# Routing attention and an MLP mixer on one core: cluster marks turned by a transposing DMA, the range check in three steps, a pair's x turned in one place

## The chip, the cores and the metric

The kernel runs on one core of a Trainium2 chip. The metric is the device time in microseconds (us), from the first instruction to the last; lower is better. Three runs of the kernel before gave 903.83, 905.47 and 905.58 us; their median, 905.47 us, is the time before.

## What is computed

Two blocks follow each other. The first is attention in which a query sees only the keys of its own cluster; the second mixes tokens and then channels. Cut to what matters:

```python
# q, k, v: (4, 8, 768, 64), 16 centroids for each head
q_assign = argmax(q_n . c_n)            # nearest of 16 centroids, k likewise
mask = q_assign[:, :, :, None] == k_assign[:, :, None, :]
scores = where(mask, (q @ k.T) / 8, -1e9)
attn = softmax(scores)
x = attn @ v                            # bridged to (4, 768, 512)
h = relu(x.T @ w_tok1) @ w_tok2         # tokens, 768 -> 256 -> 768
u = x + h.T
out = u + relu(u @ w_ch1) @ w_ch2       # channels, 512 -> 1536 -> 512
```

## The kernel before

The attention works on 16 pairs of heads (`NPAIR`), each in four steps (`GROUPS`): a step is one half of the queries (384 of 768) against three blocks of 128 keys. `m` counts the 64 steps, `g` is the pair and `s` the step in it. While pair `g` is in its scores, pair `g+1` is routed, which means that the nearest centroid of each of its queries and keys is found, and pair `g-1` is finished. Instructions run on each engine in the order in which the code gives them.

Routing compares each row's 16 similarities with their maximum. The result `oh` has rows as partitions; the scores need it turned, clusters as partitions (`ohT`). The turned marks enter the score as one more product in the same PSUM sum: a key's marks are 0 for its own cluster and -2^33 for the others, so a query of another cluster gets a score that the exponential takes to 0.

```python
    def route(g, a0=0, a1=2):

        st = state[g]
        NR = (a1 - a0) * NJ * 2
        sc = rsmall.tile([P, NR, C], F32, name="sim")
        nc.vector.transpose(
            out=sc.rearrange("p n c -> p (n c)"), in_=st.pop("pr")
        )
        mx = rsmall.tile([P, NR], F32, name="mx")
        nc.vector.reduce_max(out=mx, in_=sc, axis=AX.X)
        oh = ohs[g % 2][:, a0:a1].rearrange("p a j (h x) -> p (a j) h x", h=2)[:, :, :, 0:C]
        nc.vector.tensor_tensor(
            out=oh, in0=sc.rearrange("p (n h) c -> p n h c", h=2),
            in1=mx.rearrange("p (n h) -> p n h", h=2).unsqueeze(3).to_broadcast([P, NR // 2, 2, C]),
            op=ALU.is_ge,
        )

    def route_turn(g, a, po=None):

        st, oh = state[g], ohs[g % 2]
        if a == 1:
            st["ohT"] = qktp.tile([P, 2, NJ, P], BF16, name="ohT")
        if po is None:
            po = ps_sc.tile([P, NJ, P], BF16, tag="sc", name="po")
        for j in range(NJ):
            nc.tensor.transpose(out=po[:, j], in_=oh[:, a, j], identity=identb)
        st["po", a] = po

    def route_copy(g, a):
        st = state[g]
        po = st.pop(("po", a))
        if a == 0:
            nc.vector.tensor_copy(out=st["ohT"][:, 0], in_=po)
        else:
            nc.scalar.activation(
                out=st["ohT"][:, 1], in_=po, func=ACT.Copy, scale=BIG, bias=-BIG,
                accum_out=cells[:, g : g + 1],
            )
```

The scores of one step take three tiles of the PSUM pool `ps_sc`, which has `NG` = 3 buffers in all. The tile that is used last waits longest for its buffer, so its products come last:

```python
    def scores(m):
        g, qh, j0 = split(m)
        st = state[g]
        js = slice(HJ * qh, HJ * qh + HJ)
        scs = [ps_sc.tile([P, 2, 512], F32, tag="sc", name="sc") for _ in range(NG)]

        for chunks in (range(NG - 1), (NG - 1,)):
            for src, start in ((st["ohT"], True), (st["T"], False)):
                for i in chunks:
                    for h in range(2):
                        rows = slice(h * D, (h + 1) * D)
                        nc.tensor.matmul(
                            scs[i][:, h, 0:HS], lhsT=src[rows, 1, j0 + i], rhs=src[rows, 0, js],
                            start=start, stop=not start,
                        )
        for i in range(NG):
            ex = work.tile([P, 2, HS], F32, name="ex")
            nc.scalar.activation(out=ex, in_=scs[i][:, :, 0:HS], func=ACT.Exp, scale=SM_SCALE)
            st["ex", qh, j0 + i] = ex
```

A finished pair is turned back (`half_turn`, six transposes on PE in two halves) and divided by its sums into `x` (`half_out`, on DVE):

```python
    def half_turn(g, qh, px):
        for i in range(HJ):
            nc.tensor.transpose(
                out=px[:, i * P : i * P + P], in_=state[g]["avT"][:, HJ * qh + i], identity=ident
            )
        state[g]["px", qh] = px

    def half_out(g, qh):

        b, f = divmod(g, NF)
        nc.vector.tensor_tensor(
            out=xs[b][:, HJ * qh : HJ * qh + HJ, f * P : (f + 1) * P].rearrange(
                "p j (h d) -> p j h d", h=2
            ),
            in0=state[g].pop(("px", qh)).rearrange("p (j h d) -> p j h d", h=2, j=HJ),
            in1=rcps[:, g, qh].rearrange("p h j -> p j h").unsqueeze(3).to_broadcast([P, HJ, 2, D]),
            op=ALU.mult,
        )
# ... (half_out goes on:)
            in0=state[g].pop(("px", qh)).rearrange("p (j h d) -> p j h d", h=2, j=HJ),
            in1=rcps[:, g, qh].rearrange("p h j -> p j h").unsqueeze(3).to_broadcast([P, HJ, 2, D]),
            op=ALU.mult,
        )
```

The order of a pair's four steps (`add_up` sums the exponentials on DVE, `values` multiplies them with v on PE, `weights` holds the pieces in which the weights of the second block are prepared, on DVE, ACT and GpSimd):

```python
    for m in range(last + 3):
        g, s = divmod(m, GROUPS)
        more = g < NPAIR - 1
        old = g - 1 if m < last else -1
        if s == 2:
            if old >= 0:
                pair_denominators(old)
            if more:
                route(g + 1)
            if old >= 0:
                pair_reciprocals(old)
        if s == 3 and old >= 0:
            half_out(old, 0)
        if s == 0 and old >= 1:
            half_out(old - 1, 1)
        if more and s == 0:
            turn(g + 1)
        if 1 <= m <= last:
            add_up(m - 1)
        if m < last:
            scores(m)
        if 1 <= m <= last:
            values(m - 1)
        if m < last and s == 1:
            two = ps_sc.tile([P, 2, 512], F32, tag="sc", name="small")
            if old >= 0:
                pair_sums(old, two[:, 0, 0:HS])
            if more:
                route_products(g + 1, pr=two[:, 1, 0:HS])
        if m < last and s == 2:
            if more:
                two = ps_sc.tile([P, 2, 1024], BF16, tag="sc", name="po")
                for a in (1, 0):
                    po = two[:, a, 0 : NJ * P].rearrange("p (j t) -> p j t", j=NJ)
                    route_turn(g + 1, a, po)
                for a in (1, 0):
                    route_copy(g + 1, a)
            if old >= 0:
                half_turn(old, 0, ps_w.tile([P, HS], F32, tag="w", name="px"))
        if m < last and s == 3 and old >= 0:
            half_turn(old, 1, ps_w.tile([P, HS], F32, tag="w", name="px"))
        # ... (the end of the last pair)
        if s == 1 and g + 2 < NPAIR:
            load(g + 2)
        # ...
        if m < last - GROUPS:
            n = m % WEVERY == 0 or m == 1        # WEVERY = 3
        else:
            n = m % 2 if m < last else 2
        for _ in range(min(n, len(weights))):
            weights.pop(0)()
        # ...
```

The fast path holds for inputs in a certain range. `fits` finds out whether they were in it: 1/sum within limits, and one cluster only for each key. It counts over the partitions with a product on PE and loads the three counts into a register of every engine; if they fall short, a general version is run after the fast one.

```python

    def fits():

        inside = const.tile([P, 3, 2 * NPAIR * 2 * HJ], F32, name="inside")
        good = const.tile([P, 3], F32, name="good")
        flat = rcps.rearrange("p n i h j -> p (n i h j)")
        for i, (limit, op) in enumerate(((LIMIT, ALU.is_le), (1.0 / LIMIT, ALU.is_ge))):
            nc.vector.tensor_scalar(
                out=inside[:, i], in0=flat, scalar1=limit, scalar2=None, op0=op
            )
            nc.vector.tensor_reduce(out=good[:, i : i + 1], in_=inside[:, i], axis=AX.X, op=ALU.min)

        nc.vector.tensor_scalar(
            out=inside[:, 2, 0:NPAIR], in0=cells, scalar1=1.0 / BIG, scalar2=float(S),
            op0=ALU.mult, op1=ALU.add,
        )
        nc.vector.reduce_sum(out=good[:, 2:3], in_=inside[:, 2, 0:NPAIR], axis=AX.X)
        pn = ps_w.tile([1, 3], F32, tag="w", name="pn")
        nc.tensor.matmul(pn, lhsT=ones[:, 0:1], rhs=good, start=True, stop=True)
        count = const.tile([1, 3], I32, name="count")
        nc.vector.tensor_copy(out=count[:, 0:2], in_=pn[:, 0:2])
        nc.vector.tensor_scalar(
            out=count[:, 2:3], in0=pn[:, 2:3], scalar1=float(B * H * S), scalar2=float(P),
            op0=ALU.is_equal, op1=ALU.mult,
        )
        loaded = [
            nc.values_load(count[0:1, i : i + 1], min_val=0, max_val=P) for i in range(3)
        ]
# ... and in the second block:
            for i in range(3):
                ch2_chunk(b, part, i)
                # ...
            if b == 0 and part == 0:
                both = fits()
    late.pop()()          # the last product of the last chunk
    # ...
    with tc.If(both < 3 * P):
        general()
```

Of the kernel before, what the change touches and what calls it, by code (L numbers as in the profile page):

```python
# [8 lines left out]
F32 = mybir.dt.float32  # L9
BF16 = mybir.dt.bfloat16  # L10
U32 = mybir.dt.uint32
I32 = mybir.dt.int32
ALU = mybir.AluOpType
ACT = mybir.ActivationFunctionType
AX = mybir.AxisListType

B, H, S, D = 4, 8, 768, 64
C = 16
P = 128
# [28 lines left out]
def kernel(  # L48
# [257 lines left out]
    def route(g, a0=0, a1=2):  # L306

        st = state[g]  # L310
        NR = (a1 - a0) * NJ * 2
        sc = rsmall.tile([P, NR, C], F32, name="sim")
        nc.vector.transpose(
            out=sc.rearrange("p n c -> p (n c)"), in_=st.pop("pr")
        )
        mx = rsmall.tile([P, NR], F32, name="mx")
        nc.vector.reduce_max(out=mx, in_=sc, axis=AX.X)
        oh = ohs[g % 2][:, a0:a1].rearrange("p a j (h x) -> p (a j) h x", h=2)[:, :, :, 0:C]
        nc.vector.tensor_tensor(
            out=oh, in0=sc.rearrange("p (n h) c -> p n h c", h=2),  # L320
            in1=mx.rearrange("p (n h) -> p n h", h=2).unsqueeze(3).to_broadcast([P, NR // 2, 2, C]),
            op=ALU.is_ge,
        )

    def route_turn(g, a, po=None):

        st, oh = state[g], ohs[g % 2]
        if a == 1:
            st["ohT"] = qktp.tile([P, 2, NJ, P], BF16, name="ohT")
        if po is None:
            po = ps_sc.tile([P, NJ, P], BF16, tag="sc", name="po")
        for j in range(NJ):
            nc.tensor.transpose(out=po[:, j], in_=oh[:, a, j], identity=identb)  # L338
        st["po", a] = po

    def route_copy(g, a):
        st = state[g]
        po = st.pop(("po", a))
        if a == 0:
            nc.vector.tensor_copy(out=st["ohT"][:, 0], in_=po)  # L345
        else:
            nc.scalar.activation(
                out=st["ohT"][:, 1], in_=po, func=ACT.Copy, scale=BIG, bias=-BIG,
                accum_out=cells[:, g : g + 1],
            )  # L350


    def split(m):
# [284 lines left out]
    def ch2_chunk(b, part, i):  # L638
# [29 lines left out]

        chunk(DM // 2, product, done)

    def fits():

        inside = const.tile([P, 3, 2 * NPAIR * 2 * HJ], F32, name="inside")
        good = const.tile([P, 3], F32, name="good")
        flat = rcps.rearrange("p n i h j -> p (n i h j)")
        for i, (limit, op) in enumerate(((LIMIT, ALU.is_le), (1.0 / LIMIT, ALU.is_ge))):
            nc.vector.tensor_scalar(
                out=inside[:, i], in0=flat, scalar1=limit, scalar2=None, op0=op
            )
            nc.vector.tensor_reduce(out=good[:, i : i + 1], in_=inside[:, i], axis=AX.X, op=ALU.min)  # L680

        nc.vector.tensor_scalar(
            out=inside[:, 2, 0:NPAIR], in0=cells, scalar1=1.0 / BIG, scalar2=float(S),
            op0=ALU.mult, op1=ALU.add,
        )
        nc.vector.reduce_sum(out=good[:, 2:3], in_=inside[:, 2, 0:NPAIR], axis=AX.X)
        pn = ps_w.tile([1, 3], F32, tag="w", name="pn")
        nc.tensor.matmul(pn, lhsT=ones[:, 0:1], rhs=good, start=True, stop=True)
        count = const.tile([1, 3], I32, name="count")
        nc.vector.tensor_copy(out=count[:, 0:2], in_=pn[:, 0:2])  # L690
        nc.vector.tensor_scalar(
            out=count[:, 2:3], in0=pn[:, 2:3], scalar1=float(B * H * S), scalar2=float(P),
            op0=ALU.is_equal, op1=ALU.mult,
        )
        loaded = [
            nc.values_load(count[0:1, i : i + 1], min_val=0, max_val=P) for i in range(3)
        ]
        return loaded[0] + loaded[1] + loaded[2]


    def begin():
        cen = rsmall.tile([P, D], F32, name="cen")
        nc.sync.dma_start(cen, centroids.rearrange("h c d -> (h c) d"))
        load(0, (nc.scalar, nc.sync))

        nc.vector.memset(ones, 1.0)
        warm = rsmall.tile([P, WMAX], BF16, name="warm")
        nc.vector.memset(warm, 0.0)
        nc.scalar.activation(out=rsmall.tile([P, QP], F32, name="expd"), in_=ones, func=ACT.Exp)
        make_identity(nc, ident)  # L710
        nc.gpsimd.tensor_copy(out=identb, in_=ident)
        for oh in ohs:
            nc.gpsimd.memset(oh, 0.0)
        load(1)
        pw = ps_av.tile([P, HS], F32, name="av")

        def keep_warm(n):
            for _ in range(n):
                nc.tensor.matmul(pw, lhsT=warm[:, 0:P], rhs=warm[:, P : P + HS], start=True, stop=True)

        keep_warm(12)
        centroids_norm(cen)
        keep_warm(7)
        turn(0, (1,))
        route_products(0, 1, 2)
        turn(0, (0,))
        route(0, 1, 2)
        keep_warm(1)
        route_products(0, 0, 1)
        keep_warm(2)  # L730
        route_turn(0, 1)
        route_copy(0, 1)
        route(0, 0, 1)
        keep_warm(1)
        route_turn(0, 0)
        route_copy(0, 0)

    begin()
    weights = list(weight_steps(stage, W, ("tok1", "tok2", "ch1")))
# [7 lines left out]
# [9 lines that stand above are left out]
            if old >= 0:  # L756
                pair_reciprocals(old)
        if s == 3 and old >= 0:
            half_out(old, 0)
        if s == 0 and old >= 1:  # L760
            half_out(old - 1, 1)
        if more and s == 0:
            turn(g + 1)
        if 1 <= m <= last:
# [8 lines that stand above are left out]
                pair_sums(old, two[:, 0, 0:HS])  # L773
            if more:
                route_products(g + 1, pr=two[:, 1, 0:HS])
        if m < last and s == 2:
            if more:
                two = ps_sc.tile([P, 2, 1024], BF16, tag="sc", name="po")
                for a in (1, 0):
                    po = two[:, a, 0 : NJ * P].rearrange("p (j t) -> p j t", j=NJ)  # L780
                    route_turn(g + 1, a, po)
                for a in (1, 0):
                    route_copy(g + 1, a)
            if old >= 0:
                half_turn(old, 0, ps_w.tile([P, HS], F32, tag="w", name="px"))
        if m < last and s == 3 and old >= 0:
            half_turn(old, 1, ps_w.tile([P, HS], F32, tag="w", name="px"))
        if m == last:
            ps_sc_stack.close()
            pools["ps_m"] = pool("ps_m", 2, space=PSUM)  # L790
            half_out(NPAIR - 2, 1)
        if m == last + 1:
            pair_sums(NPAIR - 1, ps_w.tile([P, HS], F32, tag="w", name="den"))
            pair_denominators(NPAIR - 1)
            pair_reciprocals(NPAIR - 1)
            half_turn(NPAIR - 1, 0, ps_w.tile([P, HS], F32, tag="w", name="px"))
            half_turn(NPAIR - 1, 1, ps_av.tile([P, HS], F32, name="av"))
        if m == last + 2:
            for qh in range(2):
                half_out(NPAIR - 1, qh)  # L800
        if s == 1 and g + 2 < NPAIR:
            load(g + 2)
        if m == last - GROUPS:
            assert not weights
            routing.close()
            W["ch2"] = pool("wc2pool", 1, side="right").tile([P, NCT, DM], F32, name="wc2")
            weights = list(weight_steps(stage, W, ("ch2",)))
        if m < last - GROUPS:
            n = m % WEVERY == 0 or m == 1
# [4 lines that stand above are left out]
        if m >= last:  # L814
            for _ in range(3):
                ends.pop(0)()
# [15 lines left out]
    for b in range(B):  # L832
        for part in range(2):
# [5 lines left out]
            for i in range(3):  # L839
                ch2_chunk(b, part, i)  # L840
                if part == 1 and i < 2 and b + 1 < B:
                    turn_u(b + 1, i)
            if b == 0 and part == 0:
                both = fits()
    late.pop()()


    def general():
# [209 lines left out]
```

## Time and profile before

| What | Before |
|---|---|
| time, median of three runs | 905.47 us |
| span of the profiled execution | 904.5 us |
| PE busy | 887.6 us (98%) |
| DVE busy | 506.6 us (56%) |
| ACT busy | 295.8 us (33%) |
| DMA, mean over the span | 46 GB/s |

PE is TensorE's matmul unit, PEld its weight load, DVE VectorE, ACT ScalarE and SP SyncE, whose queue issues most of the transfers. The table's busy times are sums over the whole span, in which the attention (to about 357 us) and the second block follow each other. A busy time of PE includes the pipelining of its matmuls, so that one instruction's duration is longer than the distance to the next; where a step's length matters, the distance between starts is read.

### The profile page before, as it was taken

What the parts mean: (1) busy time and instruction counts of PE and PEld (TensorE: products, weight loads), DVE (VectorE), ACT (ScalarE), POOL (GpSimd) and SP (SyncE); (2) the same over time, 40 slices, a digit from 0 to 9 for tenths busy, and PEclk for the clock granted to TensorE, in tenths of its full rate; (3) what the DMA queues carried; (4) which work ended last, traced back from release to release, by engine and by line L of the source; (5) the groups of instructions that cost most, each with busy time, mean ns of one, the idle gap of its engine ahead of it and who ended that gap; (6) DMA issues with size and microseconds to landing.
All of it is one profiled execution on the core that took longest, in us unless ns stands there. A gap on an engine that the chain in (4) does not pass through costs nothing.

```text
span 904.5 us, 11304 instructions
## 1 busy us (share of the span) xinstructions
PE 887.6 (98%) x4466; PEld 530.5 (59%) x4466; DVE 506.6 (56%) x834; ACT 295.8 (33%) x500; POOL 44.7 (5%) x40
## 2 busy tenths in 40 slices
PE   7999999999999999999999899999999999999997
PEld 3444444444444444444458568687685867858676
DVE  5687787788788776385473244333443334434342
ACT  3555555565556545231120121201213022030210
POOL 1010000010101000130000000000000000000000
PEclk9999999999999999999999899999999999999999
DMA  9735434443353100230000001000010000100001
GB/s 153 159 72 100 83 91 87 77 96 80 76 100 76 64 24 25 70 116 1 0 1 1 0 12 47 12 1 1 12 47 12 1 0 13 47 12 1 1 12 62
DMA packets 112829, 41.74 MB, mean 46 GB/s; under 512 B 101632, under 2 KB 105728, under 8 KB 112768
## 3 DMA queue, kind: packets, MB, share of 16 engines
q1 hardware_dynamic: 109632, 40.55, 19.6%
q10 hardware_dynamic: 3136, 0.39, 0.3%
q8 instruction: 37, 0.61, 0.3%
q14 instruction: 24, 0.20, 0.1%
HBM read 34.64 MB, written 6.29 MB: 45 GB/s over the span
## 4 chain that ended last, share of the span: by engine, by line
PE 97%; DMA 1%; DVE 1%; ACT 0%; issue 0%
PE sc L369 18%; PE av L400 15%; PE pX L652 14%; PE pX L601 14%; PE pZ L652 7%; PE pZ L601 7%; PE ph L470 5%; PE pu L479 5%; PE pY L652 3%; PE pY L601 3%; PE po L338 1%; PE px L430 1%; PE small L417 1%; PE pt L542 1%; PE small L299 1%; DMA qk<-in_k_dram 1%
## 5 line engine op out<-in xcount | busy, mean ns | idle before, releaser
L375 ACT ACTIVATE ex<-sc 128x768 f32<-128x768 f32 x192 | 144.4, 811 | 102.7 <-PE sc L369 57.9
L369 PE MATMUL sc<-qkT 64*128 64x384 f32 x768 | 144.9, 483 | 0.0
L400 PE MATMUL av<-ex,va 128*64 128x384 f32 x768 | 138.0, 494 | 0.0
L390 DVE TENSOR_TENSOR sum<-sum,ex 128x768 f32<-128x768 f32 x128 | 124.4, 972 | 9.8 <-DVE sum L390 0.9
L400 PEld LDWEIGHTS av<-ex,va 128*64 128x64 f32 x768 | 49.4, 136 | 80.3 <-issue 71.6
L369 PEld LDWEIGHTS sc<-qkT 64*128 64x128 f32 x768 | 69.9, 188 | 35.1 <-issue 14.1
L601 PE MATMUL pX<-uT,wc 128*128 128x384 f32 x192 | 68.8, 495 | 1.6 <-issue 1.6
L609 ACT COPY p<-pX 128x384 f32<-128x384 f32 x24 | 11.4, 475 | 153.1 <-PE pX L601 153.1
L369 PE MATMUL sc<-ohT 64*128 64x384 bf16 x384 | 53.3, 328 | 0.7 <-DVE ohT L345 0.7
L601 PEld LDWEIGHTS pX<-uT,wc 128*128 128x128 f32 x192 | 36.7, 193 | 26.7 <-issue 3.3
L224 POOL TENSOR_TENSOR wc<-wT,wup 128x512 int32<-128x512 int32 x24 | 32.6, 1360 | 246.5 <-DVE wT L217 159.1
L479 PE MATMUL pu<-h,wt 128*128 128x512 f32 x96 | 42.0, 592 | 0.0
L470 PE MATMUL ph<-x,wt 128*128 128x512 f32 x96 | 42.0, 593 | 0.0
L496 DVE TENSOR_TENSOR x<-pX,x 128x256 f32<-128x256 f32 x24 | 10.2, 424 | 55.1 <-PE pX L652 55.1
L496 DVE TENSOR_TENSOR c<-pZ,u 128x384 f32<-128x384 f32 x24 | 13.4, 558 | 46.8 <-PE pZ L601 46.8
L652 PE MATMUL pX<-w2s,hA 128*128 128x256 f32 x144 | 36.4, 390 | 0.5 <-DVE x L496 0.5
L496 DVE TENSOR_TENSOR hA<-pY,p 128x384 f32<-128x384 f32 x24 | 13.4, 557 | 40.4 <-PE pY L601 40.4
L386 DVE TENSOR_TENSOR sum<-ex 128x768 f32<-128x768 f32 x32 | 34.7, 1083 | 1.5 <-ACT ex L375 1.5
L652 PE MATMUL pX<-wc,hA 128*128 128x256 f32 x144 | 35.0, 379 | 0.0
L652 PE MATMUL pZ<-w2s,hS 128*128 128x256 f32 x144 | 35.0, 379 | 0.0
L652 PE MATMUL pY<-wc,hA 128*128 128x256 f32 x144 | 35.0, 379 | 0.0
L652 PE MATMUL pX<-w2s,hS 128*128 128x256 f32 x144 | 35.0, 379 | 0.0
(123 smaller groups left out, 1195.2 us busy)
## 6 DMA issues: line engine op xcount, KB each, us to landing
raw<-in_moe_w_ch_dram SPq DMA_DIRECT2D x24, 512.0 KB, 3.9
qk<-in_k_dram SPq DMA_DIRECT2D x64, 96.0 KB, 4.5
va<-in_v_dram SPq DMA_DIRECT2D x16, 384.0 KB, 3.2
out_dram<-x SPq DMA_DIRECT2D x24, 256.0 KB, 2.0
qk<-in_q_dram SPq DMA_DIRECT2D x60, 96.0 KB, 3.5
raw<-in_moe_w_tok_dram SPq DMA_DIRECT2D x3, 512.0 KB, 5.7
raw<-in_moe_w_tok_dram SPq DMA_DIRECT2D x4, 384.0 KB, 3.9
qk<-in_q_dram ACTq DMA_DIRECT2D x4, 96.0 KB, 4.7
```

The source lines that it names most:

```text
L224: nc.gpsimd.tensor_tensor(out=dst.bitcast(I32), in0=T, in1=up, op=ALU.add)
L369: nc.tensor.matmul(scs[i][:, h, 0:HS], lhsT=src[rows, 1, j0 + i], rhs=src[rows, 0, js], start=start, stop=not start,)
L375: nc.scalar.activation(out=ex, in_=scs[i][:, :, 0:HS], func=ACT.Exp, scale=SM_SCALE)
L386: nc.vector.tensor_tensor(out=acc, in0=e[0], in1=e[1], op=ALU.add)
L390: nc.vector.tensor_tensor(out=acc, in0=acc, in1=ex, op=ALU.add)
L400: nc.tensor.matmul(st["av"][h * D : (h + 1) * D], lhsT=st["va"][:, h, j], rhs=ex[:, h], start=(j == 0), stop=(j == NJ - 1),)
L470: nc.tensor.matmul(pf, lhsT=W["tok1"][:, j, t * P : (t + 1) * P], rhs=xs[b][:, j], start=(j == 0), stop=(j == NJ - 1),)
L479: nc.tensor.matmul(pu, lhsT=W["tok2"][:, t, j], rhs=h1s[b][:, t], start=(t == 0), stop=(t == NT - 1))
L496: nc.vector.tensor_tensor(out=dst, in0=a, in1=b, op=ALU.add)
L601: nc.tensor.matmul(psum, lhsT=A[a][:, k, c * P : (c + 1) * P], rhs=R[r][:, k], start=start and k == 0, stop=k == 1, skip_group_check=not s ...
L609: nc.scalar.copy(out=kept[name], in_=psum)
L652: nc.tensor.matmul(psum, lhsT=h2[a][:, k, i * P : (i + 1) * P], rhs=Bw[w][:, 3 * part + k], start=start and k == 0, stop=k == 2, skip_grou ...
```

## The change

The cluster marks of pairs 1 to 15 are turned by one transposing DMA for each pair, from SBUF to SBUF, in place of twelve transposes on PE and the two copies out of PSUM. [...] DVE writes the final values first: 1 or 0 times -2^33 for the queries (`a` = 0), and "below the maximum" as 1 or 0 for the keys (`a` = 1). ACT counts the keys' marks in a pass of its own. Pair 0, which nothing runs ahead of, is still turned on PE. As the PSUM tile `po` is no longer there, its place in `ps_sc` is given to both halves of `x`, which are now turned together in step 2 and taken out together at the head of step 3. The range check is cut in three: the comparisons on DVE after the first part of image 0, the product on PE after the second part, and the register loads at the end of the kernel.

```diff
--- before.py
+++ after.py
@@ -307,6 +307,9 @@
 
 
 
+
+
+
         st = state[g]
         NR = (a1 - a0) * NJ * 2
         sc = rsmall.tile([P, NR, C], F32, name="sim")
@@ -315,39 +318,44 @@
         )
         mx = rsmall.tile([P, NR], F32, name="mx")
         nc.vector.reduce_max(out=mx, in_=sc, axis=AX.X)
-        oh = ohs[g % 2][:, a0:a1].rearrange("p a j (h x) -> p (a j) h x", h=2)[:, :, :, 0:C]
-        nc.vector.tensor_tensor(
-            out=oh, in0=sc.rearrange("p (n h) c -> p n h c", h=2),
-            in1=mx.rearrange("p (n h) -> p n h", h=2).unsqueeze(3).to_broadcast([P, NR // 2, 2, C]),
-            op=ALU.is_ge,
+        for a in range(a0, a1):
+            oh = ohs[g % 2][:, a].rearrange("p j (h x) -> p j h x", h=2)[:, :, :, 0:C]
+            n = slice((a - a0) * 2 * NJ, (a - a0 + 1) * 2 * NJ)
+            nc.vector.tensor_tensor(
+                out=oh, in0=sc[:, n].rearrange("p (j h) c -> p j h c", h=2),
+                in1=mx[:, n].rearrange("p (j h) -> p j h", h=2).unsqueeze(3)
+                .to_broadcast([P, NJ, 2, C]),
+                op=ALU.is_lt if a else ALU.is_ge,
+            )
+            if a:
+                nc.scalar.activation(
+                    out=rsmall.tile([P, NJ, 2, C], BF16, name="others"), in_=oh, func=ACT.Copy,
+                    accum_out=cells[:, g : g + 1],
+                )
+            else:
+                nc.vector.tensor_scalar_mul(out=oh, in0=oh, scalar1=-BIG)
+
+    def route_turn(g):
+
+        st = state[g]
+        st["ohT"] = qktp.tile([P, 2, NJ, P], BF16, name="ohT")
+        nc.sync.dma_start_transpose(
+            out=st["ohT"].rearrange("p a j t -> p (a j) t"),
+            in_=ohs[g % 2].rearrange("p a j x -> p (a j x)"),
         )
 
-    def route_turn(g, a, po=None):
-
-
-
-
-
-
-        st, oh = state[g], ohs[g % 2]
+    def route_turn_first(a):
+
+        st, oh = state[0], ohs[0]
         if a == 1:
             st["ohT"] = qktp.tile([P, 2, NJ, P], BF16, name="ohT")
-        if po is None:
-            po = ps_sc.tile([P, NJ, P], BF16, tag="sc", name="po")
+        po = ps_sc.tile([P, NJ, P], BF16, tag="sc", name="po")
         for j in range(NJ):
             nc.tensor.transpose(out=po[:, j], in_=oh[:, a, j], identity=identb)
-        st["po", a] = po
-
-    def route_copy(g, a):
-        st = state[g]
-        po = st.pop(("po", a))
         if a == 0:
             nc.vector.tensor_copy(out=st["ohT"][:, 0], in_=po)
         else:
-            nc.scalar.activation(
-                out=st["ohT"][:, 1], in_=po, func=ACT.Copy, scale=BIG, bias=-BIG,
-                accum_out=cells[:, g : g + 1],
-            )
+            nc.scalar.copy(out=st["ohT"][:, 1], in_=po)
 
 
     def split(m):
@@ -668,30 +676,32 @@
 
         chunk(DM // 2, product, done)
 
+    good = const.tile([P, 3], F32, name="good")
+    count = const.tile([1, 3], I32, name="count")
+
     def fits():
 
+
         inside = const.tile([P, 3, 2 * NPAIR * 2 * HJ], F32, name="inside")
-        good = const.tile([P, 3], F32, name="good")
         flat = rcps.rearrange("p n i h j -> p (n i h j)")
-        for i, (limit, op) in enumerate(((LIMIT, ALU.is_le), (1.0 / LIMIT, ALU.is_ge))):
-            nc.vector.tensor_scalar(
-                out=inside[:, i], in0=flat, scalar1=limit, scalar2=None, op0=op
-            )
-            nc.vector.tensor_reduce(out=good[:, i : i + 1], in_=inside[:, i], axis=AX.X, op=ALU.min)
-
-        nc.vector.tensor_scalar(
-            out=inside[:, 2, 0:NPAIR], in0=cells, scalar1=1.0 / BIG, scalar2=float(S),
-            op0=ALU.mult, op1=ALU.add,
-        )
-        nc.vector.reduce_sum(out=good[:, 2:3], in_=inside[:, 2, 0:NPAIR], axis=AX.X)
+        for i, (src, limit, op) in enumerate(
+            (
+                (flat, LIMIT, ALU.is_le),
+                (flat, 1.0 / LIMIT, ALU.is_ge),
+                (cells, float(2 * NJ * (C - 1)), ALU.is_equal),
+            )
+        ):
+            ok = inside[:, i, 0 : src.shape[1]]
+            nc.vector.tensor_scalar(out=ok, in0=src, scalar1=limit, scalar2=None, op0=op)
+            nc.vector.tensor_reduce(out=good[:, i : i + 1], in_=ok, axis=AX.X, op=ALU.min)
+
+    def fits_count():
         pn = ps_w.tile([1, 3], F32, tag="w", name="pn")
         nc.tensor.matmul(pn, lhsT=ones[:, 0:1], rhs=good, start=True, stop=True)
-        count = const.tile([1, 3], I32, name="count")
-        nc.vector.tensor_copy(out=count[:, 0:2], in_=pn[:, 0:2])
-        nc.vector.tensor_scalar(
-            out=count[:, 2:3], in0=pn[:, 2:3], scalar1=float(B * H * S), scalar2=float(P),
-            op0=ALU.is_equal, op1=ALU.mult,
-        )
+        nc.vector.tensor_copy(out=count, in_=pn)
+
+    def fits_load():
+
         loaded = [
             nc.values_load(count[0:1, i : i + 1], min_val=0, max_val=P) for i in range(3)
         ]
@@ -728,12 +738,10 @@
         keep_warm(1)
         route_products(0, 0, 1)
         keep_warm(2)
-        route_turn(0, 1)
-        route_copy(0, 1)
+        route_turn_first(1)
         route(0, 0, 1)
         keep_warm(1)
-        route_turn(0, 0)
-        route_copy(0, 0)
+        route_turn_first(0)
 
     begin()
     weights = list(weight_steps(stage, W, ("tok1", "tok2", "ch1")))
@@ -756,9 +764,8 @@
             if old >= 0:
                 pair_reciprocals(old)
         if s == 3 and old >= 0:
-            half_out(old, 0)
-        if s == 0 and old >= 1:
-            half_out(old - 1, 1)
+            for qh in range(2):
+                half_out(old, qh)
         if more and s == 0:
             turn(g + 1)
         if 1 <= m <= last:
@@ -773,22 +780,15 @@
                 pair_sums(old, two[:, 0, 0:HS])
             if more:
                 route_products(g + 1, pr=two[:, 1, 0:HS])
-        if m < last and s == 2:
-            if more:
-                two = ps_sc.tile([P, 2, 1024], BF16, tag="sc", name="po")
-                for a in (1, 0):
-                    po = two[:, a, 0 : NJ * P].rearrange("p (j t) -> p j t", j=NJ)
-                    route_turn(g + 1, a, po)
-                for a in (1, 0):
-                    route_copy(g + 1, a)
-            if old >= 0:
-                half_turn(old, 0, ps_w.tile([P, HS], F32, tag="w", name="px"))
-        if m < last and s == 3 and old >= 0:
-            half_turn(old, 1, ps_w.tile([P, HS], F32, tag="w", name="px"))
+        if more and s == 2:
+            route_turn(g + 1)
+        if m < last and s == 2 and old >= 0:
+            two = ps_sc.tile([P, 2, 512], F32, tag="sc", name="px")
+            for qh in range(2):
+                half_turn(old, qh, two[:, qh, 0:HS])
         if m == last:
             ps_sc_stack.close()
             pools["ps_m"] = pool("ps_m", 2, space=PSUM)
-            half_out(NPAIR - 2, 1)
         if m == last + 1:
             pair_sums(NPAIR - 1, ps_w.tile([P, HS], F32, tag="w", name="den"))
             pair_denominators(NPAIR - 1)
@@ -840,9 +840,10 @@
                 ch2_chunk(b, part, i)
                 if part == 1 and i < 2 and b + 1 < B:
                     turn_u(b + 1, i)
-            if b == 0 and part == 0:
-                both = fits()
+            if b == 0:
+                (fits_count if part else fits)()
     late.pop()()
+    both = fits_load()
 
 
     def general():

```

## The prediction

> **What bounds the kernel now.** I read the page first (busy times, then the chain that ended last), then the timeline of a pair, engine by engine.
>
> ```profile
> PE 887.6 (98%) x4466; PEld 530.5 (59%) x4466; DVE 506.6 (56%) x834; ACT 295.8 (33%) x500; POOL 44.7 (5%) x40
> ...
> PE 97%; DMA 1%; DVE 1%; ACT 0%; issue 0%
> ```
>
> PE is busy almost throughout, and the chain is PE for 97%. Time is won only by taking work or waits from PE, and any new wait of PE is paid in full. One pair in PE's timeline, from its step 2 on (first column: start, second: length with pipelining; I use distances between starts):
>
> ```profile
> 152.25 0.50 PE L369 MATMUL sc<-ohT 64*128 64x384 bf16 x4
> ...
> 154.78 2.16 PE L400 MATMUL av<-ex,va 128*64 128x384 f32 x12
> 156.87 0.84 PE L338 MATMUL po<-identb,oh 128*128 128x128 bf16 x12
> 157.55 0.50 PE L430 MATMUL px<-ident,avT 128*128 128x128 f32 x3
> 157.98 0.50 PE L369 MATMUL sc<-ohT 64*128 64x384 bf16 x4
> ...
> 159.60 0.33 PE L369 MATMUL sc<-ohT 64*128 64x384 bf16 x2
> ...
> 173.73 0.50 PE L369 MATMUL sc<-ohT 64*128 64x384 bf16 x4
> ```
>
> Scores take 2.53 us (154.78 - 152.25), values 2.09, the twelve turns 0.68 (157.55 - 156.87), the first three turns of x 0.43; a pair 21.48 (173.73 - 152.25). Every step of every pair shows the same 2.53 and 2.09, so PE doesn't stall here. DVE in step 2 of the next pair, one that also prepares weights:
>
> ```profile
> 173.87 0.58 DVE L421 STREAM_TRANSPOSE dent<-small 128x384 f32<-128x384 f32 x1 [3.48 <-PE small L299]
> 174.37 0.54 DVE L313 STREAM_TRANSPOSE sim<-small 128x384 f32<-128x384 f32 x1
> 174.95 0.55 DVE L317 TENSOR_REDUCE mx<-sim 128x24 f32<-128x384 f32 x1
> 175.53 0.56 DVE L319 TENSOR_TENSOR oh<-sim,mx 128x384 bf16<-128x384 f32 x1
> 176.01 0.22 DVE L424 RECIPROCAL rcps<-dent 128x12 f32<-128x12 f32 x1
> 176.15 3.02 DVE L390 TENSOR_TENSOR sum<-sum,ex 128x768 f32<-128x768 f32 x3
> 180.16 0.56 DVE L345 COPY ohT<-po 128x768 bf16<-128x768 bf16 x1 [0.99 <-ACT ohT L347]
> 180.63 0.42 DVE L207 TENSOR_SCALAR wh<-wh 128x512 f32<-128x512 f32 x1
> ...
> 182.22 0.55 DVE L438 TENSOR_TENSOR x<-px,rcps 128x384 f32<-128x384 f32 x1
> ```
>
> DVE waits for PE (3.48 us) before `dent`; from there it is a serial chain locked to the start of step 2 (173.73). The copy that frees `po` ends 6.99 us after that start. The third tile of step 3's scores takes that buffer, and its first product comes 7.35 us after (159.60 - 152.25): it fits, with 0.36 to spare, because the copy stands ahead of the weights. The one real hole of PE is in the second block:
>
> ```profile
> 497.78 1.46 PE L652 MATMUL pX<-wc,hS 128*128 128x256 f32 x6
> 501.15 0.19 PE L688 MATMUL pn<-good,ones 128*1 128x3 f32 x2 [1.91 <-DVE good L686]
> 502.93 2.90 PE L601 MATMUL pX<-uT,wc 128*128 128x384 f32 x4 [1.59 <-issue]
> 505.62 2.75 PE L652 MATMUL pX<-w2s,hA 128*128 128x256 f32 x6
> 508.18 1.48 PE L601 MATMUL pZ<-uTs,w1s 128*128 128x384 f32 x4
> ```
>
> PE waits for DVE's comparisons, then for its register loads, and the two groups behind them last 2.69 and 2.56 us where such groups otherwise take 1.29: from 499.00 to 510.40 the mean granted clock was 0.70.
>
> **What the Trainium skill says.** (1) "VectorE: DVE Perf Modes", section "The three transpose paths": a 128x128 bf16 block takes 390 ns on TensorE and 1309 ns by DMA. In this trace twelve such blocks take PE 0.68 us, 57 ns each, because they follow each other in the pipeline; the DMA figure no run here shows yet. (2) "DMA: Bandwidth & Descriptors", section "Latency and other measured facts": a transposing DMA moved 261 GB/s in one kernel; not shown here either. For a plain transfer the trace has 3.2 us to landing for the 384 KB of `va`. (3) "TensorE: Matmul & The Clock Gate", section "What's actually happening": an idle window of about 3.4 us brings the half clock. The trace agrees: PE did next to nothing from 499.07 to 502.93 and came back at half clock.
>
> **Part 1: turns by DMA.** Fifteen pairs lose 0.68 us of PE: -10.2 us. x turned in one go saves the second change-over: single turns start 0.11 us apart, so six take about 0.48 + 3 x 0.11 = 0.81 us instead of 0.43 + 0.48; 15 x 0.10 = -1.5. ACT loses 0.81 + 0.19 us per pair for a smaller pass, off the path. DVE's one comparison of 0.56 us becomes two over half the elements (0.36 each, as pair 0's L319 shows) and a scaling between them (0.25, as L677 takes for 192 elements): by starts 0.40 + 0.22 + 0.30 = 0.92 us instead of 0.48, so what stands behind comes 0.44 later. The marks are final about 1.80 + 0.92 + 0.1 = 2.8 us after the start of step 2.
>
> Does the DMA land in time? The next pair starts 4.62 (step 2) + 0.81 (turns of x) + 4.62 (step 3) = 10.05 us after that start, so 7.2 us are left. It moves 128 x 1536 x 2 B = 393 KB. Estimate from page (2): 1.5 us at 261 GB/s, plus the 1.7 us in which the 32 KB of the centroids landed: 3 to 5 us with the issue. SP's own queue is not in the way: its loads run a pair ahead. I take it as hidden, with doubt: twelve blocks in series at the 1309 ns of page (1) would be 15.7.
>
> **Part 2: x in one place.** Here I see a new wait. The third tile of step 3's scores now takes the buffer of both halves of x. Two `half_out` on DVE free it, and they stand behind the three sums and, in some pairs, behind a step of weights. PE wants it at 4.62 + 0.81 + 1.62 = 7.05 us. DVE: the sums start at 2.42 + 0.44 = 2.86 and end at 5.88; two `half_out`, 0.47 apart and 0.55 long, end at 6.90. That just fits. With weights between, add 1.59 us (182.22 - 180.63): freed at 8.5, and PE waits some 1.5 us. Weights fall in step 2 where m = 4g + 2 is a multiple of 3: m = 6, 18, 30, 42 and 54, five pairs. Sum: 5 x 1.55 = +7.7 us. A gap of 1.5 us should not halve the clock.
>
> **Part 3: the range check.** From 497.78 to 508.18 are 10.40 us for three groups of 1.29: 6.5 us lost to waits and clock. With the comparisons one part earlier, `pn` finds its input ready: -6.5 + 0.1. The register loads go to the end, where SP is last: three loads with their arithmetic held SP from 501.55 to 503.5, so +1.9 behind the issue of the last output. Pair 0's scaling lies bare at the start: +0.3.
>
> **Sum:** 905.5 - 10.2 - 1.5 + 7.7 - 6.4 + 1.9 + 0.3 = 897.3. A little for the doubt in the DMA: 898.
>
> **The rivals.**
> - *No wait for x's buffer.* If the buffers fall otherwise, or DVE gets there first, the 7.7 us are kept: 890. For it: without weights the chain fits by 0.15 us. Against it: the chain on DVE starts only when PE lets it, and in all five pairs with weights the first `half_out` comes 8.5 us after step 2's start, in the others 6.9.
> - *The DMA lands late.* Then PE waits at the head of each of 15 pairs: 2 us too late is up to +30 us, 925; at 15.7 us it is 15 x 8 or more, and the clock falls too: over 1020. For it: no transposing DMA is in this trace, and rows of 256 B are many small pieces. Against it: transfers of 384 KB land here in 3 to 4 us.
> - *DVE becomes the bound.* It gains 0.44 us in the chain but loses the 0.56 us copy, and it idles 1.0 and 3.5 us ahead of `dent` in the two pairs shown: no more than noise.
>
> **Range and chances.** The check (-4.2 with start and tail) and the turns (-11.7) are fairly sure; the five waits give half back. 890 is the case without them. Upward is the DMA: one in six or so for a lateness that matters. Range 889 to 920. Two per cent below is 887.4, more than I can add up even without new waits; two per cent above is 923.6. Faster by over 2%: 0.10; within: 0.76; slower: 0.14.
>
> **What would show it.** Right: `po` in pair 0 only, pairs of 20.7 us and five of 22.2; in those five the second `sc<-ohT` group of step 3 starts 1.5 us late, released by `half_out`; the transposing DMA lands within 7.2 us and PE's first scores of a pair don't wait for it; around 499 us no hole and full clock; three register loads on SP behind the last output. Part 2 is wrong if no pair is longer, part 1 if each pair begins with a wait. Most wrong would be a DMA so slow that PE's gaps halve the clock.

## The result and the profile after

The changed kernel takes 896.2 us (median; 895.07 to 897.53) against 905.46 us before: ratio 0.9902, 95% interval 0.9881 to 0.9924. The prediction was 898 us, range 889 to 920.

The page of the changed kernel: the busy times, and the chain that ended last, whose 5% for DVE are new.

```profile
PE 873.7 (98%) x4286; PEld 519.4 (58%) x4286; DVE 499.4 (56%) x849; ACT 286.4 (32%) x501; POOL 44.6 (5%) x40
...
PE 93%; DVE 5%; DMA 1%; ACT 0%; issue 0%; DVEq 0%
```

PE lost 180 transposes (4466 - 4286) and 13.9 us of busy time. That the chain now runs over DVE for 5% says that PE waits for DVE somewhere. PE's timeline in steps 2 and 3 of a pair whose step 2 has weights (start, length, then the group; in brackets the idle time ahead and its releaser):

```profile
171.45 0.50 PE L377 MATMUL sc<-ohT 64*128 64x384 bf16 x4
...
173.97 2.16 PE L408 MATMUL av<-ex,va 128*64 128x384 f32 x12
176.06 0.88 PE L438 MATMUL px<-ident,avT 128*128 128x128 f32 x6
176.87 0.50 PE L377 MATMUL sc<-ohT 64*128 64x384 bf16 x4
177.21 1.45 PE L377 MATMUL sc<-qkT 64*128 64x384 f32 x8
179.79 0.34 PE L377 MATMUL sc<-ohT 64*128 64x384 bf16 x2 [1.13 <-DVE x L446]
```

`po` is gone from this pair, and the six turns of x take 0.81 us (176.87 - 176.06). The second `sc<-ohT` group of step 3 comes 2.92 us after the first, where it was 1.62: the wait of part 2, released by `half_out` (L446). DVE in the same stretch shows why:

```profile
173.65 0.21 DVE L336 TENSOR_SCALAR oh<-oh 128x192 bf16<-128x192 bf16 x1
173.77 0.35 DVE L324 TENSOR_TENSOR oh<-sim,mx 128x192 bf16<-128x192 f32 x1
...
174.18 3.02 DVE L398 TENSOR_TENSOR sum<-sum,ex 128x768 f32<-128x768 f32 x3
177.12 0.42 DVE L207 TENSOR_SCALAR wh<-wh 128x512 f32<-128x512 f32 x1
177.57 0.43 DVE L212 TENSOR_SCALAR wh<-wh 128x512 uint32<-128x512 uint32 x1
178.11 0.69 DVE L217 SCALAR_TENSOR_TENSOR wT<-raw,wh 128x512 uint32<-128x512 uint32 x1
178.72 1.01 DVE L446 TENSOR_TENSOR x<-px,rcps 128x384 f32<-128x384 f32 x2
```

The two `half_out` stand behind three operations on weights, for which only GpSimd is waiting, off the chain. PE waits so in five pairs, for 1.28, 1.02, 1.30, 1.29 and 1.29 us, together 6.2. The other pairs take 20.69 us (from step 2 at 66.96 to step 2 at 87.65, for one) and show no wait. From the answer on the tile `ohT`, the transposing DMA and its landing:

```profile
L342 SPq DMA_TRANSPOSE ohT<-oh x15: 1327/1474/1579, 27.4 to 322.9; - x15
...
DMA to landing us min/median/max: 3.7/3.7/4.1
```

It lands in 3.7 us, and no engine has a wait for it in the list of waits. In the second block, PE at the two places of the check, first where the comparisons now run on DVE, then where the product `pn` stands:

```profile
492.90 1.46 PE L660 MATMUL pX<-wc,hS 128*128 128x256 f32 x6
494.19 1.45 PE L609 MATMUL pX<-uT,wc 128*128 128x384 f32 x4
495.48 1.46 PE L660 MATMUL pX<-w2s,hA 128*128 128x256 f32 x6
496.78 1.45 PE L609 MATMUL pZ<-uTs,w1s 128*128 128x384 f32 x4
```
```profile
550.84 1.46 PE L660 MATMUL pX<-wc,hS 128*128 128x256 f32 x6
552.23 0.19 PE L700 MATMUL pn<-good,ones 128*1 128x3 f32 x2
552.35 1.56 PE L609 MATMUL pX<-uT,wc 128*128 128x384 f32 x4
553.74 1.46 PE L660 MATMUL pX<-w2s,hA 128*128 128x256 f32 x6
```

The three groups that took 10.40 us take 3.88 (496.78 - 492.90), at full clock. `pn` costs 0.3: the two groups around it take 2.90 us (553.74 - 550.84) instead of twice 1.29. The register loads stand at the end (per engine: shortest, median and longest in ns, then first and last start):

```profile
L706 PEldq TENSOR_LOAD <-count x3: 305/309/490, 886.2 to 887.2; - x3
...
L706 SPq TENSOR_LOAD <-count x3: 261/283/526, 888.6 to 890.1; - x3
```

DVE's last addition, in the kernel before and in the changed one:

```profile
898.87 0.42 DVE L496 TENSOR_TENSOR x<-pX,x 128x256 f32<-128x256 f32 x1 [1.66 <-PE pX L652]
```
```profile
887.75 0.42 DVE L504 TENSOR_TENSOR x<-pX,x 128x256 f32<-128x256 f32 x1 [1.66 <-PE pX L660]
```

From there to the end of the span (895.3) are 7.5 us; before (904.5), they were 5.6.

The account of the two profiled spans, by starts in PE's timeline, 904.5 to 895.3: up to step 2 of pair 0 +0.9 us, from there to the first product of the second block -5.8 (332.95 to 327.16), the second block -6.2 (541.31 to 535.07), the end +1.9.

### The profile page after: what moved, and what is told of

Its sections match the earlier page's. It is cut to its first block, busy times and chain, and to the rows that moved or that the text cites. A ratio compares the mean times of both kernels' runs of the same rounds, so it can differ in the third digit from the quotient of the medians.

```text
span 895.3 us, 11001 instructions
## 1 busy us (share of the span) xinstructions
PE 873.7 (98%) x4286; PEld 519.4 (58%) x4286; DVE 499.4 (56%) x849; ACT 286.4 (32%) x501; POOL 44.6 (5%) x40
## 4 chain that ended last, share of the span: by engine, by line
PE 93%; DVE 5%; DMA 1%; ACT 0%; issue 0%; DVEq 0%
PE sc L377 16%; PE pX L660 14%; PE pX L609 14%; PE av L408 14%; PE pZ L660 7%; PE pZ L609 7%; PE ph L478 5%; PE pu L487 5%; PE pY L660 3%; PE pY L609 3%; DVE sum L398 2%; PE small L425 1%; PE pt L550 1%; PE small L299 1%; PE px L438 1%; DMA qk<-in_k_dram 1%
## 5 line engine op out<-in xcount | busy, mean ns | idle before, releaser
L377 PEld LDWEIGHTS <-ohT 64*128 64x128 bf16 x384 | 13.8, 94 | 49.0 <-issue 32.2
L429 DVE STREAM_TRANSPOSE dent<-small 128x384 f32<-128x384 f32 x15 | 8.7, 583 | 55.9 <-PE small L299 50.5
L504 DVE TENSOR_TENSOR x<-pX,x 128x256 f32<-128x256 f32 x24 | 10.2, 424 | 49.3 <-PE pX L660 49.3
```

Of the source, the lines that this page charges most:

```text
L377: nc.tensor.matmul(scs[i][:, h, 0:HS], lhsT=src[rows, 1, j0 + i], rhs=src[rows, 0, js], start=start, stop=not start,)
L504: nc.vector.tensor_tensor(out=dst, in0=a, in1=b, op=ALU.add)
```

## Experiments

Theory A is the prediction's sum: turns -11.7, waits for x's buffer +6.2 as now measured, check -4.5 with its tail (-4.6 in the first expectation). That makes -10.0; the spans show -9.2, since the start of the profiled run took 0.9 us longer. Rivals: B, the whole gain is the check; C, the five long pairs come from the amount of DVE's work, not from its order; D, the register loads themselves, and not the waits around them, made the hole in PE. Ratios are to the kernel before, run beside them.

| Kernel | Median us | Ratio, 95% interval |
|---|---|---|
| changed kernel | 896.2 | 0.9881 to 0.9924 |
| check in three steps only | 901.24 | 0.9940 to 0.9967 |
| turns by DMA only | 896.15 | 0.9882 to 0.9912 |
| changed, x in two places | 892.59 | 0.9843 to 0.9873 |
| changed, x out first | 890.56 | 0.9824 to 0.9851 |
| changed, loads in the middle | 895.15 | 0.9881 to 0.9911 |
| x out first, one load | 889.07 | 0.9816 to 0.9843 |
| x out first, turned twice | 894.45 | 0.9878 to 0.9914 |
| x out first, turned thrice | 984.86 | 1.0877 to 1.0928 |
| one load, more filling at the start | 887.73 | 0.9791 to 0.9817 |
| one load, in the middle | 887.15 | 0.9792 to 0.9819 |
| all of it | 886.92 | 0.9787 to 0.9815 |

### The check alone

The kernel before, with the check cut in three:

```diff
-            if b == 0 and part == 0:
-                both = fits()
+            if b == 0:
+                (fits_count if part else fits)()
     late.pop()()
+    both = fits_load()
```

> The kernel before with only the range check cut in three. Theory A (the gain of 9.3 us is the sum of three terms: turns -11.7, waits for x's buffer +6.2, check -4.6): 905.5 - 6.5 + 0.1 + 1.9 = 901.0 us; no hole of PE around 499 us, full clock there, and SP's three register loads behind the last output. Theory B (the whole gain is the check, and turning by DMA is worth nothing): 896 us.

901.24 us, 4.2 less than before. PE at the place of the former hole:

```profile
498.29 1.46 PE L652 MATMUL pX<-wc,hS 128*128 128x256 f32 x6
499.58 1.46 PE L601 MATMUL pX<-uT,wc 128*128 128x384 f32 x4
500.87 1.46 PE L652 MATMUL pX<-w2s,hA 128*128 128x256 f32 x6
```

Groups 1.29 us apart, no wait. A holds; B falls, since the check explains less than half of the gain.

### The turns alone

The changed kernel with x as before and the check as before in one place:

```diff
-            two = ps_sc.tile([P, 2, 512], F32, tag="sc", name="px")
-            for qh in range(2):
-                half_turn(old, qh, two[:, qh, 0:HS])
+            half_turn(old, 0, ps_w.tile([P, HS], F32, tag="w", name="px"))
+        if m < last and s == 3 and old >= 0:
+            half_turn(old, 1, ps_w.tile([P, HS], F32, tag="w", name="px"))
 # ... half_out(old, 0) at s == 3, half_out(old - 1, 1) at s == 0
-                (fits_count if part else fits)()
+                fits(); fits_count(); both = fits_load()   # b == 0, part == 0
```

> Only the turns by DMA: x is turned and taken out in two places as before, and the check stands in one place as before. Theory A: 15 x 0.68 us of PE are gone and nothing is added, 905.5 - 10.2 = 895.3 us; pairs of 20.8 us, all alike. Theory B: 905 us.

896.15 us, 9.2 less than before. PE from one step 2 to the next, without most of the groups that lie between:

```profile
106.85 0.50 PE L377 MATMUL sc<-ohT 64*128 64x384 bf16 x4
...
111.46 0.55 PE L438 MATMUL px<-ident,avT 128*128 128x128 f32 x3
111.94 0.50 PE L377 MATMUL sc<-ohT 64*128 64x384 bf16 x4
...
116.55 0.55 PE L438 MATMUL px<-ident,avT 128*128 128x128 f32 x3
117.03 0.50 PE L377 MATMUL sc<-ohT 64*128 64x384 bf16 x4
...
127.69 0.50 PE L377 MATMUL sc<-ohT 64*128 64x384 bf16 x4
```

Pairs of 20.84 us (127.69 - 106.85) instead of 21.48, all alike: 0.64 less each, not 0.68, since the first three turns of x now take 0.48 (111.94 - 111.46) instead of 0.43. The turns alone bring as much as the whole change, so the other two parts together gave nothing: the gain of the check was eaten by the waits for x's buffer.

### x back in two places

The changed kernel with only the part on x undone (the first half of the edit above).

> The changed kernel with x turned and taken out in two places as before. Theory A: the five waits (6.2 us) go and the second change-over comes back (15 x 0.10 = 1.5), 896.2 - 6.2 + 1.5 = 891.5 us. Theory C (the five long pairs come from DVE having too much to do in them, wherever x is taken out): about 896 us, with five pairs still longer than the others.

892.59 us, 3.6 less than the change itself, and no pair is longer than the others (20.84 us each). Step 3 of a pair with weights, PE and then DVE:

```profile
174.97 0.50 PE L377 MATMUL sc<-ohT 64*128 64x384 bf16 x4
...
176.59 0.33 PE L377 MATMUL sc<-ohT 64*128 64x384 bf16 x2
```
```profile
176.53 0.69 DVE L217 SCALAR_TENSOR_TENSOR wT<-raw,wh 128x512 uint32<-128x512 uint32 x1
177.14 0.55 DVE L446 TENSOR_TENSOR x<-px,rcps 128x384 f32<-128x384 f32 x1
```

DVE still does the weights ahead of `half_out`, but the third tile comes at its usual 1.62 us after the first (176.59 - 174.97): C falls. Of the 1.1 us above the expectation, 0.8 are the second change-over, which costs 0.15 us for each pair (20.84 - 20.69) and not 0.10. Giving x the freed place in the pool was a loss as it stands.

### x out ahead of the weights

```diff
-        if s == 3 and old >= 0:
-            for qh in range(2):
-                half_out(old, qh)
 # ...
             for qh in range(2):
                 half_turn(old, qh, two[:, qh, 0:HS])
+            for qh in range(2):
+                half_out(old, qh)
```

> The changed kernel with both halves of x taken out at the end of step 2, ahead of the step of weights on DVE, instead of at the head of step 3. Theory A: x's buffer is free about 6.9 us after the start of step 2 and PE wants it at 7.05, so all five waits go: 896.2 - 6.2 = 890.0 us, all pairs 20.7. Theory C: DVE still has the same work, so the wait moves to another place: 895 to 896 us.

890.56 us. The same work in another order, in a pair with weights, DVE and then PE:

```profile
171.35 3.02 DVE L398 TENSOR_TENSOR sum<-sum,ex 128x768 f32<-128x768 f32 x3
174.29 1.02 DVE L446 TENSOR_TENSOR x<-px,rcps 128x384 f32<-128x384 f32 x2
175.22 0.42 DVE L207 TENSOR_SCALAR wh<-wh 128x512 f32<-128x512 f32 x1
```
```profile
174.04 0.50 PE L377 MATMUL sc<-ohT 64*128 64x384 bf16 x4
...
175.67 0.33 PE L377 MATMUL sc<-ohT 64*128 64x384 bf16 x2
```

x's buffer is free at 175.31, and the third tile starts at its usual 1.63 us (175.67 - 174.04). All five waits are gone, and the median is 5.6 us lower, of the 6.2 expected. This is A in its plainest form: only the order changed.

### The register loads in the middle

```diff
                 (fits_count if part else fits)()
+            if b == 1 and part == 0:
+                both = fits_load()
     late.pop()()
-    both = fits_load()
```

> The changed kernel with the three register loads not at the end but after the first part of image 1, when the counts have long been there. Theory A: the 6.5 us of the check in one place were two waits of PE and the low clock that followed; with nothing to wait for, the loads hold PE for about 1.3 us (501.56 to 502.90 in the kernel before) and leave the clock up, and the end loses its 1.9 us: 896.2 + 1.3 - 1.9 = 895.6 us. Theory D (the loads into registers are themselves what broke PE's flow): 896.2 + 6.5 - 1.9 = 900.8 us, with low clock behind them.

895.15 us. D falls: no low clock and no hole. A's figure was met, but one of its terms was wrong. The loads of PE, and PE's groups around them:

```profile
L706 PEldq TENSOR_LOAD <-count x3: 306/309/495, 604.3 to 605.3; - x3
```
```profile
603.63 1.46 PE L660 MATMUL pZ<-wc,hS 128*128 128x256 f32 x6
604.92 1.46 PE L660 MATMUL pX<-wc,hS 128*128 128x256 f32 x6
606.22 1.45 PE L609 MATMUL pX<-uT,wc 128*128 128x384 f32 x4
```

The loads run from 604.3 to 605.6 and PE's groups stay 1.29 us apart: they cost PE nothing, not 1.3 us. The second block is as long as with the loads at the end (535.07 us in both). The end shrinks from 7.5 to 5.7 us. Of the 1.9 us that this should bring the medians show 1.1; the scatter of the changed kernel's own runs is 2.5 us.

### One load

```diff
             nc.vector.tensor_reduce(out=good[:, i : i + 1], in_=ok, axis=AX.X, op=ALU.min)
+        nc.vector.tensor_reduce(out=every, in_=good, axis=AX.X, op=ALU.min)
 # ... pn is [1, 1], from every; one values_load; both < P
```

> The kernel that takes x out first (890.6 us) with the three counts brought down to one on DVE before the product on PE, so that only one register load stands at the end. Theory A: SP's stretch behind the last output shrinks from 2.0 to about 0.75 us, 890.6 - 1.25 = 889.3 us. If the loads are hidden behind the landing of the last output, it stays at 890.6.

889.07 us, 1.5 less. From DVE's last addition (879.38) to the end (885.7) are 6.3 us instead of 7.5: the loads at the end are paid, not hidden behind the last output's landing.

### The DMA made twice, and thrice

These two ask how far the DMA is from the path. They repeat it into the same tile:

```diff
+        for _ in range(2):        # 3 in the second
             nc.sync.dma_start_transpose(
```

> The kernel that takes x out first (890.6 us) with each pair's transposing DMA made twice, one after the other, into the same tile; the second waits for the first. Theory A (the DMA is hidden, with 10.05 - 2.8 = 7.2 us against its 3.7): two end 2.8 + 2 x 3.7 = 10.2 us or a little later after the start of step 2, so PE waits 0.2 to 0.5 us at the head of 15 pairs: 893 to 898 us. If the DMA slows PE by its mere traffic, it shows as longer steps all over.

> The same with three transposing DMAs in a row for each pair. Theory A: the third lands 2.8 + 3 x 3.7 = 13.9 us after the start of step 2, 3.9 us late, 15 times: 890.6 + 58 = 949 us, and [...] up to 45 us more. If PE had more room than reckoned, less than 20 us.

894.45 and 984.86 us. PE's waits for this DMA (in us: total, times, longest), with two and then with three:

```profile
PE sc L378 <- DMA ohT<-oh: 4.0, 5, 1.2
```
```profile
PE sc L378 <- DMA ohT<-oh: 59.9, 15, 5.1
```

With two, the first list leaves out the short waits: by starts, PE is late at the head of all 15 pairs, ten times by 0.05 to 0.2 us and five times by 0.4 to 1.25, some 5.2 us together. Why five are longer is open. The median rose by 3.9, the span by 3.5, because the start of this profiled run was 1.7 us quicker; no other step grew longer. With three, the head of a pair whose gap was among the longest:

```profile
146.48 0.82 PE L378 MATMUL sc<-ohT 64*128 64x384 bf16 x4 [5.14 <-DMA ohT<-oh]
147.10 2.77 PE L378 MATMUL sc<-qkT 64*128 64x384 f32 x8
```

And its window from 100 to 340 us: busy time of PE, PEld, DVE, ACT and GpSimd, then granted clock, DMA share and GB/s.

```profile
100.00:340.00 240.00, 204.94 (x1264) 90.82 (x1260) 149.32 (x225) 103.38 (x165) 16.15 (x12) 0.89 0.60 114
```

PE waits for the DMA, and after 14 of the 15 gaps, which last 3.65 to 5.1 us, the clock falls to half for a while (2.77 us for a group of 1.45; 0.89 in the mean). The rise is 94 us: 60 are the waits, where 15 x 3.9 = 58 was reckoned, and the other 34 or so came with the low clock. So the one DMA is hidden with about 3.6 us to spare (10.05 less 2.7 to its issue and 3.7 to its landing), and the reckoning of the slack was right to 0.1 us: two in series just miss.

### The start, and all together

In the profiles, the recorded mean clock of the first 20 us is 0.74 in the changed kernel and 1.00 in the one before; others show 0.83 or 0.91. The 1.00 doesn't mean full speed throughout: the first routing products took 0.87 us in the kernel before (first line) and 0.53 in the kernel with more filling (second line), and both record 1.00.

```profile
10.66 0.87 PE L299 MATMUL pr<-qkT,cnd 128*32 128x192 f32 x8 [1.89 <-DVE qkT L287]
```
```profile
10.58 0.53 PE L299 MATMUL pr<-qkT,cnd 128*32 128x192 f32 x8
```

More filling products of PE ahead of pair 0:

```diff
-        keep_warm(7)
+        keep_warm(15)
```

> The kernel with one load (889.1 us) with 15 instead of 7 idle-filling products of PE ahead of pair 0, against the gap of 2.5 us in which PE waits for the first keys. In the profiles so far the mean clock of the first 20 us was 0.74 in some and 1.00 in others. If that gap decides it, the clock is 1.00 here and the time comes to the lower end of the kernel with one load, 887.5 to 888 us with less scatter; if not, 889.

887.73 us against 889.07, with a spread of 1.2 us instead of 2.0 and a recorded clock of 1.00; but the profile of the kernel with one load, its fastest run (887.53), also had 1.00. Step 2 of pair 0 starts at 23.1 us here, and with 7 products anywhere from 22.9 to 25.1, so the additional products spare the slow starts and don't beat a quick one. The mean clock of the whole runs agrees: 0.998 or more in all eleven runs with 15 products (these and those of "all of it"), 0.993 to 1.000 in the ten with 7 and one load, and there the slower runs have the lower clock. That the gap of 2.5 us is what decides it is likely and not shown.

> The kernel with one load (889.1 us) with that load after the first part of image 1. The end loses its last 0.75 us, PE pays one load of about 0.5 us: 888.8 us, not to be told from 889.1.

887.15 us, 1.9 below the load at the end instead of 0.3. The end gains 0.7 us, PE loses nothing; the remaining 1.2 lie within the scatter of the two kernels (886.74 to 888.77 and 887.53 to 889.54).

> All that helped in one kernel: x out first, one load after the first part of image 1, 15 filling products at the start. From 887.2 us with the load in the middle, less up to 0.5 us if the start matters: 886.5 to 887.2 us. If the filling products only delay pair 0 when the clock is up anyway, 887.2 to 887.6.

886.92 us, ratio 0.9801: the lowest median, 9.3 us below the changed kernel. One of its six executions took 4917.91 us, for a reason that isn't known; the other five have a median of 886.71 (886.26 to 887.91). That doesn't tell it apart from one load in the middle (886.74 to 888.77).

## Why the prediction was right

**Part 1 (turns) was right.** Pairs without a wait take 20.69 us, predicted 20.7; six turns of x 0.81, as worked out. That two terms met so well is in part luck: the turns gave 0.64 for each pair instead of 0.68, x in one go 0.15 instead of 0.10. The DMA lands in 3.7 us, predicted 3 to 5, with 7.2 at hand; the two parts of that estimate, bytes and fixed time, were not measured apart. The twice and thrice runs show that this slack is real. The 1309 ns per block of the Trainium skill ("VectorE: DVE Perf Modes", section "The three transpose paths") did not add up in series: twelve blocks in one DMA take 3.7 us, not 15.7.

**Part 2 (x in one place) was right in mechanism, large by a fifth.** The five waits came where they were placed and nowhere else, but for 1.24 us in the mean instead of 1.55, +6.2 instead of +7.7. The term that was mis-sized is DVE's delay, in two places: the scaling of the marks overlaps the next comparison (173.77 is only 0.12 us after its start at 173.65, not 0.22), so the sums begin 2.73 us after step 2 and not 2.86; and the sums were counted by their length, 3.02 us, where the next operation starts after 2.94 (177.12 - 174.18). The weights pass in 1.60 us as before, and x's buffer is free 8.3 us after the start, not 8.5. That is 0.21 of the 0.31 us by which the mean wait is shorter. The clock stayed at 1.00 in the 5 us after each of the five waits, as predicted.

**Part 3 (check) was right.** -6.5 for the hole, +0.3 for `pn` where 0.1 was reckoned, +1.9 for the loads at the end; -4.2 by itself in the run with the check alone, where -4.5 without the start's 0.3 was reckoned. The start was the weak term: pair 0's scores began 0.27 us earlier, not 0.3 later, and its first steps were 1.2 us slower in the profiled run, with a low clock there. The start differs as much between kernels that have it in common (22.9 to 25.1 us to step 2 of pair 0), so this is hardly the change's.

**The sum.** 897.3 was reckoned and 898 forecast. The errors are of both signs: waits -1.5, `pn` +0.2, start of the profiled run +0.6. The distance from 897.3 to 896.2 is within the kernel's own scatter (895.07 to 897.53), so the median can't say which of them counts.

**The rivals.** That x's buffer would cause no wait fell, and the run with x out first shows what it would have been worth: 890.56, where the rival said 890. The late DMA didn't come, and the run with three shows what it would have cost; the 925 named for a lateness of 2 us should by the prediction's own sum have been 927 (897.3 + 30). DVE is not the bound: in the 14 waits for the routing products ahead of `dent` it now idles 50.5 us instead of 28.5.

## What to carry to other kernels

On a kernel bound by one engine, work handed to a DMA is won almost in full (here 9.2 of 10.2 us) as long as the DMA lands before its reader; write down both times, and try the slack by making the DMA twice. A buffer that a change gives to something new brings a new releaser: look at what stands in front of it in that engine's order, and put urgent releases ahead of work that can wait. A wait of PE that is long enough costs twice, once for the wait and once for the clock afterwards (here the 3.9 us around `pn` and 14 of the 15 gaps of 3.65 us and more, but none of the five of about 1.3), so checks belong where their input is long ready.

## What the runs showed of the hardware

Register loads on PE in mid-stream cost the matmuls nothing when their value was ready (groups 1.29 us apart right through), while at the end each costs SP some 0.6 us in full. A transposing DMA of 393,216 bytes from SBUF to SBUF held SP's queue 1.47 us to issue and landed after 3.7, close to the 3.2 of the plain load of `va` in the same kernel, which has as many bytes (the profile's 384 KB). And the twelve turns on PE that it replaced had cost 0.68 us: the DMA is five times slower and still the better place, because nobody waits for it.
